# Decay columns by SBUF rows and TensorE, a first block in two groups, and another order of the steps, in a gated linear recurrence with a feed-forward layer

## The chip, the cores and the metric

The kernel runs on one core of a Trainium2 chip. The metric is the device time of one execution in microseconds, the median of several runs; profiles are of one execution each. TensorE (PE) multiplies matrices into PSUM, which has eight banks here. VectorE (DVE), ScalarE (ACT) and GpSimd (POOL) do the elementwise work, SyncE (SP) issues most of the DMAs. Each engine works through its own queue in order.

## The reference

```python
mag = sqrt(a_re*a_re + a_im*a_im)
scale = minimum(mag, 0.999) / (mag + 1e-06)
a_re_n, a_im_n = a_re*scale, a_im*scale
for t in range(S):                       # S = 768
    ar, ai = a_re_n[:, :, t, :, None], a_im_n[:, :, t, :, None]
    new_re = ar*S_re - ai*S_im
    new_im = ar*S_im + ai*S_re
    S_re, S_im = new_re + k[t] (x) v[t], new_im       # outer product, per head
    y[:, :, t] = q[t] @ S_re
x = y, tokens as rows                    # 4 x 768 tokens, 8 heads x 48 = 384 columns
out = (sigmoid(x @ w_gate) * (x @ w_val)) @ w_out     # 384 -> 1536 -> 384
```

There are 4 batches, 8 heads and 48 channels. a is complex, one number for each channel and token.

## The kernel before, in words

The sequence is cut into six blocks of 128 tokens. A slab is one batch in one block, numbered m = 4 x block + batch, so slabs 0 to 3 are the first block, and there are 24. Within a slab the recurrence becomes matrix products: logarithms of the magnitudes and angles are summed along the tokens by a matmul with a triangular matrix; k and q are multiplied by the exponentials and by cosine and sine; q times k gives a masked score matrix, and scores times v give y. A state for each batch carries from block to block, and is multiplied by the decay over a whole block, a number for each channel.

Slabs are prepared in groups, `SIZES` (4, 4, 4, 4, 4, 2, 2). Each piece of work is a step with a name, and `Plan.order` sorts all steps by the due times in the table `TIMES`, then puts them out in that order. So the table is the order of each engine's queue; its numbers do nothing else. `HOME` says by a letter for each step of a kind whether it runs on VectorE (v), GpSimd (g) or ScalarE (a). `SLOTS` gives the buffers, `WARM` puts extra matmuls on zeros ahead of some steps. ScalarE's function tables are loaded where the order needs another one.

The steps, by name:

- per slab: lr, la load a; sq squares it, add adds the two squares; lk, lq, lv load k, q, v; v16 converts v.
- per group: lna (Ln of the real part), inv (Exp of its negative), r (imaginary over real), atan (Arctan); lnm (Ln of the magnitude), lh the cap on it. Groups in `SPLIT` make fp16 pairs (lh, ll; th, tl) in place of fp32 for the two triangular matmuls.
- per slab: cl (triangular matmul of the logarithms), ee (its two exponentials), qke (q and k times ee); ct (triangular matmul of the angles, with the carried angle), r16 and nid (whole turns off), cr (the carry), ab, cs (the two sines); ks, qs (k and q times cosine and sine); tp and qkT (transposes of k and q by TensorE and the copy from PSUM), or xk and xq for slabs in `CROSSED` (the DMA crossbar); sc (scores), mst (mask); kv and P (state update), u (state times decay), x16 (its fp16 copy); y, y16, xp, xt (output, fp16, transposed).
- per pair of slabs: pg and pv (the two feed-forward products, six pieces each, L1058), tanh and p (the gate), po (second product, L1097); then ot and st (evacuation and store).

What the change touches is the way of the block's decay from one row to columns. The last token's row of ee, 384 numbers on one partition, goes to DRAM by scr (L691). When all rows of a group are there, rbe (L698) reads them back by two DMAs with channels on partitions, 48 at partition 0 and 48 at partition 64:

```python
nc.sync.dma_start(
    rbe[p0:p0 + D, c, lo:lo + n],
    scr[c][lo:lo + n].rearrange("b (h d) -> d b h", d=D))
```

Then arr (L707, GpSimd) multiplies a block's columns by those of the block before. u (L955) multiplies the state by arr.

Of the kernel before, what the change touches and what calls it, by code (L numbers as in the profile page):

```python
# [10 lines left out]
ALU = mybir.AluOpType  # L11
# [16 lines left out]
CROSSED = range(9, 24)  # L28
# [3 lines left out]
SPLIT = range(2, 7)  # L32
MSTP = ()
HOME = {
    "sq": "vaaavvvaaaaaaaavaaaaaaaa",
    "add": "vgvvgggggggggggggggggvgg",
    "lh": "gvgggggvvggv",
    "r": "vvgggggggggv",
    "v16": "ggggggvvggggggagvvvavagv",
    "qke": "gggvggggggggggggggggvggg",  # L40
    "th": "aaaavgggvgav",
    "ab": "vaavvaaavaaavvaaaaaaaavv",
    "u": "ggggggggggggggggvvvv",
    "x16": "gggvgaagggvavggg",
    "y16": "vaavavvvaavvavvvaaaaaaaa",
    "xt": "vvavvvvvavvvvvvavavaavav",
    "ot": "avvvaavvavaaavavaavavaaav",
}
SIZES = [4, 4, 4, 4, 4, 2, 2]
TIMES = {  # L50
    "wg": [
        28.88, 44.09, 23.19],
    "wv": [
        31.95, 49.27, 52.96],
    "wo": [
        74.01, 69.87, 76.44],
    "lr": [
        0.75, 10.04, 8.57, 1.12, 10.05, 13.69, 19.93, 24.8, 44.13, 57.38,
        60.18, 62.71, 70.64, 78.81, 78.82, 70.65, 101.57, 120.18, 117.75,
        117.48, 166.56, 168.43, 133.38, 151.46],  # L60
    "la": [
        1.49, 10.03, 8.56, 8.08, 13.7, 10.06, 15.09, 30.65, 47.51, 55.33,
        60.17, 62.72, 70.68, 76.47, 78.45, 78.83, 102.43, 102.49, 117.76,
        107.79, 167.59, 169.97, 134.14, 150.84],
    "sq": [
        7.2, 10.07, 8.67, 8.09, 16.38, 16.39, 19.94, 31.68, 50.55, 58.76,
        60.19, 65.28, 76.49, 78.87, 86.27, 79.55, 103.09, 122.49, 117.77,
        118.73, 171.82, 172.15, 146.69, 151.47],
    "add": [
        8.07, 12.17, 9.54, 8.55, 19.27, 23.18, 31.71, 31.73, 57.18, 63.7,  # L70
        66.74, 66.92, 78.78, 80.37, 92.65, 85.96, 116.2, 126.77, 120.19,
        123.7, 174.48, 175.13, 150.64, 154.3],
    "lna": [
        10.75, 32.78, 65.3, 92.67, 122.97, 176.29, 156.77],
    "lh": [
        12.18, 10.02, 31.66, 31.96, 70.62, 71.44, 98.38, 107.93, 127.81,
        132.62, 179.91, 158.47],
    "lnm": [
        13.71, 32.8, 67.09, 92.7, 127.39, 176.21, 155.21],
    "inv": [  # L80
        12.16, 32.79, 66.3, 92.68, 123.68, 186.68, 160.83],
    "r": [
        14.55, 13.68, 35.36, 35.47, 70.36, 69.88, 102.45, 97.5, 132.59,
        136.16, 188.77, 175.22],
    "cl": [
        17.66, 19.25, 16.37, 15.08, 34.36, 36.17, 41.65, 37.98, 74.07, 75.45,
        78.44, 77.72, 106.6, 105.21, 109.33, 109.12, 135.26, 140.18, 137.85,
        138.18, 181.4, 181.73, 172.62, 160.4],
    "ee": [
        20.75, 21.83, 19.91, 19.26, 41.31, 40.19, 42.81, 41.66, 75.49, 78.85,  # L90
        79.54, 81.56, 108.45, 107.58, 111.51, 109.52, 145.1, 141.4, 140.29,
        141.38, 182.09, 185.02, 176.12, 163.91],
    "scr": [
        32.77, 40.65, 33.65, 41.29, 56.14, 54.7, 49.68, 54.71, 97.53, 88.7,
        86.74, 98.31, 120.16, 123.71, 120.2, 119.68, 150.82, 156.06, 154.25,
        145.08, 191.39, 191.37, 187.65, 179.98],
    "rbe": [
        57.33, 57.39, 98.35, 123.74, 159.31, 200.77, 187.66],
    "lk": [
        19.92, 32.76, 24.68, 21.22, 45.82, 32.81, 49.69, 49.67, 70.66, 86.77,  # L100
        88.69, 98.36, 98.32, 109.16, 125.87, 124.61, 143.56, 98.4, 144.41,
        150.81, 154.27, 187.62, 166.15, 179.69],
    "lq": [
        24.69, 36.86, 30.66, 21.81, 47.5, 42.79, 57.37, 56.15, 76.46, 89.5,
        97.49, 98.41, 98.34, 117.95, 133.31, 124.81, 146.68, 149.99, 166.12,
        152.53, 174.3, 193.31, 179.92, 187.68],
    "lv": [
        23.15, 40.64, 24.67, 33.18, 63.3, 65.89, 76.45, 78.84, 86.76, 97.54,
        100.02, 114.29, 97.52, 133.34, 133.35, 133.82, 157.18, 163.85, 145.05,
        143.75, 196.08, 185.51, 185.52, 201.23],  # L110
    "v16": [
        23.16, 44.12, 31.69, 40.2, 65.29, 65.9, 81.57, 82.21, 102.48, 97.55,
        117.03, 117.49, 117.74, 135.3, 138.51, 140.52, 158.46, 164.82, 174.26,
        166.14, 200.58, 212.8, 200.59, 203.07],
    "qke": [
        24.7, 38.63, 31.7, 21.82, 47.52, 49.28, 58.49, 57.34, 83, 92.66,
        98.39, 99.11, 114.28, 120.21, 133.32, 130.11, 149.81, 154.26, 166.17,
        170.31, 207.38, 195.9, 186.67, 192],
    "atan": [
        17.67, 37.87, 70.84, 102.47, 140.28, 188.79, 179.95],  # L120
    "ct": [
        19.9, 22.34, 18.61, 21.23, 38.62, 42.78, 47.29, 53.38, 79.53, 82.2,
        91.02, 95.63, 110.3, 115.66, 128.44, 122.96, 145.04, 149.23, 162.25,
        163.23, 205.57, 199.59, 185.16, 186.14],
    "r16": [
        20.74, 23.98, 21.21, 22.55, 40.66, 44.71, 49.29, 55.35, 80.39, 82.99,
        93.51, 96.84, 111.3, 117.78, 130.73, 123.75, 145.86, 150.03, 163.24,
        163.84, 205.61, 200.81, 185.68, 186.66],
    "nid": [
        21.8, 28.01, 24.81, 23.14, 41.28, 45.8, 52.13, 55.54, 81.38, 84.69,  # L130
        93.94, 97.48, 111.5, 118.2, 131.37, 127.38, 146.89, 150.63, 163.89,
        166.75, 205.66, 201.64, 186.46, 187.63],
    "cr": [
        23.2, 35.46, 25.06, 24.66, 42.8, 49.24, 57.19, 57.35, 84.66, 91.36,
        97.58, 99.61, 114.27, 120.17, 132.12, 130.09, 149.01, 154.24, 166.76,
        169.5],
    "ab": [
        23.17, 36.83, 31.67, 23.9, 44.08, 46.65, 54.68, 57.2, 82.51, 91.37,
        97.56, 98.51, 112.3, 118.69, 131.73, 130.08, 147.74, 152.52, 166.13,
        170.32, 205.94, 202.02, 187.13, 191.38],  # L140
    "cs": [
        23.89, 36.85, 31.72, 25.46, 45.01, 49.25, 58.48, 57.36, 84.67, 91.38,
        98.37, 99.62, 114.32, 120.96, 132.6, 130.1, 150.83, 154.28, 166.77,
        171.8, 205.95, 203.08, 188.29, 192.65],
    "ks": [
        24.79, 39.92, 31.74, 26.65, 48.59, 49.66, 59.54, 57.59, 84.68, 93.5,
        98.44, 99.97, 116.18, 120.97, 134.13, 132.13, 151.57, 157.16, 167.58,
        174.28, 207.39, 203.34, 191.35, 193.83],
    "qs": [
        25.66, 39.93, 31.75, 28, 49.26, 51.13, 66.73, 61.47, 85.39, 93.95,  # L150
        99.1, 102.21, 116.21, 121.61, 136.15, 132.14, 152.44, 157.17, 169.49,
        174.29, 208.03, 205.62, 191.36, 194.7],
    "tp": [
        26.64, 28.02, 40.18, 40.63, 31.93, 33.19, 30.19, 30.64, 49.88, 50.33,
        61.45, 52.29, 68.26, 70.63, 64.78, 63.69, 88.06, 86.96],
    "qkT": [
        27.39, 28.87, 41.3, 41.67, 32.57, 33.64, 35.35, 31.94, 50.53, 52.97,
        62.09, 54.69, 70.67, 73.22, 66.72, 65.24, 88.85, 88.71],
    "sc": [
        28.89, 31.65, 45.79, 44.72, 35.56, 35, 36.81, 32.58, 53.21, 59.55,  # L160
        62.81, 55.32, 72.09, 80.38, 67.86, 66.91, 96.61, 89.49, 102.2, 103.48,
        117.94, 117.47, 108.78, 111.28, 125.86, 125.64, 134.12, 133.89,
        149.55, 146.67, 149, 141.36, 161.6, 166.11, 163.9, 163.94, 176.11,
        174.25, 179.67, 178.15, 214.75, 214.32, 209.97, 212.79, 197.41,
        196.54, 200.56, 201.24],
    "mst": [
        29.47, 34.24, 46.25, 45.83, 36.82, 36.84, 37.26, 35.45, 55.34, 60.16,
        63.29, 56.11, 78.8, 80.76, 69.85, 69.84, 97.51, 92.69, 104.82, 105.55,
        120.14, 118.22, 111.29, 111.7, 127.15, 130.12, 134.64, 135.25, 151.48,
        147.72, 149.8, 142.24, 162.59, 167.57, 165.19, 164.83, 179.68, 177.51,  # L170
        180.09, 179.97, 215.82, 214.74, 211.5, 213.59, 200.78, 198.31, 202.03,
        201.63],
    "kv": [
        32.75, 45.02, 41.08, 52.74, 74.04, 66.7, 85.43, 95.43, 104.35, 107.57,
        117.73, 118.71, 143.53, 139.97, 149.78, 141.15, 171.76, 168.21,
        180.55, 176.13],
    "P": [
        33.17, 45.81, 44.1, 53.2, 75.48, 67.22, 88.72, 96.62, 107.95, 108.8,
        125.22, 119.67, 145.07, 144.42, 150.86, 144.4, 174.32, 168.61, 181.75,
        179.96],  # L180
    "y": [
        35.34, 52.95, 39.91, 41.45, 65.88, 66.29, 85.49, 85.97, 103.07,
        106.19, 121.6, 118.72, 132.83, 136.14, 152.51, 152.46, 168.42, 166.57,
        182.06, 183.12, 217.78, 216.07, 201.29, 205.6],
    "y16": [
        37.86, 55.55, 41.32, 42.03, 66.71, 69.83, 86.26, 86.73, 104.59,
# [199 lines left out]
def kernel(  # L386
# [184 lines left out]
    for g, n in enumerate(SIZES):  # L571
# [131 lines left out]
        for s in range(n):  # L703
            rbe_key[m0 + s] = key
# [462 lines left out]
```

## Time and profile before

| | before |
|---|---|
| median of 3 runs | 260.3 us (259.03 to 261.05) |
| the profiled execution: own time | 259.69 us |
| its span | 258.0 us |
| mean granted TensorE clock | 0.987 |
| TensorE matmul busy, share | 218.9 us, 85% |
| VectorE, ScalarE, GpSimd busy | 82%, 78%, 51% |
| bytes moved by DMA | 40.26 MB, mean 156 GB/s |
| table loads on ScalarE (in order) | 29, 1.283 us each |

The span is the time from the first to the last instruction of the profile; the execution's own time holds some 1.7 us more. Times in the profile's rows are from the start of the span. In the view by slices each digit is the busy share in tenths of a fortieth of the span. In the view by stage each engine has its busy time and, in brackets, the number of instructions; the last three columns are the granted clock, the DMA share and GB/s. In the view of waits the row is engine, tile and line, then what it waited for, the total, the times and the longest one. Matmuls are pipelined, so their busy times overlap the next one's.

### The profile page before, as it was taken

The numbers are of one execution on the slowest core, as the hardware profiler recorded it, in microseconds if no ns is written. First come the engines' busy times: TensorE is split into PE (matmuls) and PEld (weight loads), VectorE is DVE, ScalarE is ACT, GpSimd is POOL, SyncE is SP. The second block draws the span as 40 slices with busy tenths as digits, with TensorE's granted clock in tenths as the row PEclk, the third lists the DMA queues.
The fourth block names the chain that finished last, engine by engine and source line by source line (L and its number), as shares of the span: only waits on it lengthen the run. The fifth ranks groups of instructions, "written<-read, shape, count | busy, mean of one in ns | idle before, by whom it ended". The sixth has DMA issues, their size and how long they took to land.

```text
span 258.0 us, 5947 instructions
## 1 busy us (share of the span) xinstructions
PE 218.9 (85%) x2249; PEld 168.2 (65%) x2249; DVE 210.4 (82%) x345; ACT 200.8 (78%) x323; POOL 131.0 (51%) x137
## 2 busy tenths in 40 slices
PE   0068278999999869979999899989999999999994
PEld 0034264677888647757767778768667877668882
DVE  3465699899999989997899998988897979868261
ACT  1695999966999669997899997899899894542620
POOL 3229568716996764795979931722924371000000
PEclk9999689999999999999999999999999999999999
DMA  7999994899999968998989799959999659490021
GB/s 147 216 212 197 202 178 76 141 166 117 189 186 188 193 128 147 160 231 191 213 124 218 140 166 207 222 124 110 227 147 227 112 106 163 92 196 31 3 93 61
DMA packets 182988, 40.26 MB, mean 156 GB/s; under 512 B 175880, under 2 KB 182960, under 8 KB 182960
## 3 DMA queue, kind: packets, MB, share of 16 engines
q1 hardware_dynamic: 178816, 36.33, 76.0%
q0 software_dynamic: 4144, 3.56, 9.3%
q8 instruction: 17, 0.28, 0.5%
q14 instruction: 11, 0.09, 0.1%
HBM read 30.77 MB, written 4.78 MB: 138 GB/s over the span
## 4 chain that ended last, share of the span: by engine, by line
PE 29%; DVE 17%; ACT 17%; DMA 16%; issue 8%; SPq 7%; POOL 4%; DVEq 0%; ACTq 0%; POOLq 0%
PE banks L1058 12%; PE banks L1097 8%; ACT L1130 4%; DMA qk<-in_q_dram 4%; DMA a<-in_a_re_dram 3%; DVE p L1076 3%; DMA qkT<-qst 3%; SPq L565 3%; ACT g L1069 3%; DMA v<-in_v_dram 3%; DVE mst L941 2%; SPq L698 2%; DVE kst L864 2%; PE banks L671 2%; DVE qst L864 2%
## 5 line engine op out<-in xcount | busy, mean ns | idle before, releaser
L1058 PE MATMUL banks<-xt,wv 128*128 128x256 f16 x432 | 57.2, 272 | 1.8 <-ACT ot L525 0.9
L1058 PE MATMUL banks<-xt,wg 128*128 128x256 f16 x432 | 55.9, 272 | 1.4 <-DVE p L1076 0.6
L1097 PE MATMUL banks<-wo,p 128*128 128x384 f16 (+1 forms) x300 | 55.6, 319 | 0.5 <-ACT ot L525 0.5
L1069 ACT ACTIVATE g<-banks 128x512 f16<-128x512 f32 x72 | 41.1, 601 | 18.4 <-DVE p L1076 12.5
L1076 DVE SCALAR_TENSOR_TENSOR p<-g,banks 128x512 f16<-128x512 f16 x72 | 48.0, 681 | 8.2 <-ACT g L1069 3.6
L736 POOL TENSOR_TENSOR qk<-qk,ee 128x768 f32<-128x768 f32 x22 | 41.9, 1921 | 13.5 <-DMA qk<-in_q_dram 10.9
L1058 PEld LDWEIGHTS <-wv 128*128 128x128 f16 x432 | 41.0, 98 | 10.0 <-issue 3.6
L1058 PEld LDWEIGHTS <-wg 128*128 128x128 f16 x432 | 41.3, 98 | 9.3 <-issue 2.9
L1097 PEld LDWEIGHTS <-p 128*128 128x128 f16 x300 | 27.9, 97 | 15.3 <-issue 2.1
L1130 ACT ACT_TABLE_LOAD x29 | 37.2, 1283 | 0.5
L604 POOL TENSOR_TENSOR lm<-sq 128x384 f32<-128x384 f32 x20 | 21.5, 1076 | 31.1 <-ACT sq L596 27.0
L941 DVE TENSOR_TENSOR mst<-banks,msk_t 128x512 f16<-128x512 f32 x48 | 32.1, 683 | 4.2 <-PE banks L926 4.1
L864 DVE TENSOR_TENSOR kst<-qk,banks 128x768 f16<-128x768 f32 x24 | 22.7, 947 | 4.1 <-issue 2.0
L671 PE MATMUL banks<-lm,wl_t 128*128 128x384 f32 x16 | 8.6, 653 | 17.3 <-ACT lm L617 15.5
L864 DVE TENSOR_TENSOR qst<-qk,banks 128x768 f16<-128x768 f32 x24 | 22.7, 946 | 0.0
L596 ACT ACTIVATE sq<-a 128x768 f32<-128x768 f32 x19 | 16.0, 847 | 8.0 <-DMA a<-in_a_im_dram 4.4
L660 POOL TENSOR_TENSOR a<-a 128x768 f32<-128x768 f32 x9 | 16.3, 1814 | 6.5 <-PE banks L796 3.3
L926 PEld LDWEIGHTS <-qkT 128*128 128x128 f16 x192 | 13.5, 98 | 7.0 <-issue 3.9
L671 PEld LDWEIGHTS banks<-lm,wl_t 128*128 128x128 f32 x16 | 3.6, 250 | 19.5 <-ACT lm L617 16.5
L811 DVE TENSOR_SCALAR r<-banks 128x384 f16<-128x384 f32 x24 | 13.1, 551 | 3.9 <-PE banks L796 3.3
L828 ACT ACTIVATE cr<-banks 32x384 f32<-32x384 f32 x20 | 9.7, 483 | 8.5 <-DVE banks L843 8.2
L907 PE MATMUL banks<-idn_t,kst 128*128 128x128 f16 x72 | 10.4, 229 | 6.7 <-DVE qst L864 4.6
(90 smaller groups left out, 421.9 us busy)
## 6 DMA issues: line engine op xcount, KB each, us to landing
a<-in_a_re_dram SPq DMA_DIRECT2D x24, 192.0 KB, 4.0
a<-in_a_im_dram SPq DMA_DIRECT2D x24, 192.0 KB, 3.7
qk<-in_k_dram SPq DMA_DIRECT2D x24, 192.0 KB, 3.9
qk<-in_q_dram SPq DMA_DIRECT2D x24, 192.0 KB, 2.8
v<-in_v_dram SPq DMA_DIRECT2D x24, 192.0 KB, 5.2
out_dram<-ot SPq DMA_DIRECT2D x23, 192.0 KB, 2.5
wg<-in_moe_w_gate_dram POOLq DMA_DIRECT2D x3, 384.0 KB, 7.4
wv<-in_moe_w_val_dram POOLq DMA_DIRECT2D x3, 384.0 KB, 5.4
```

What stands on the lines that cost most here:

```text
L596: on.activation(out=T[SQ], in_=T[A][:, :, s], func=FT.Square)
L604: home("add", m).tensor_tensor(out=T[LM][:, s], in0=T[SQ][:, 0], in1=T[SQ][:, 1], op=ALU.add)
L660: home("r", w).tensor_tensor(out=T[A][:, 1, i:j], in0=T[A][:, 1, i:j], in1=T[A][:, 0, i:j], op=ALU.mult)
L671: nc.tensor.matmul(T[CL][:, :HD], wl_t, T[LM][:, s], start=True, stop=True)
L736: home("qke", m).tensor_tensor(out=T[QK], in0=T[QK], in1=T[EE], op=ALU.mult)
L864: nc.vector.tensor_tensor(out=T[SL][i].rearrange("p h (r x) -> p h r x", r=2)[:, :, :, 0:D], in0=heads(T[QK][:, i]).unsqueeze(2) .broadcas ...
L941: nc.vector.tensor_tensor(out=T[MS][:, :n_], in0=T[SC], in1=msk_t.unsqueeze(1).broadcast_to([L, n_, L]), op=ALU.mult)
L1058: nc.tensor.matmul(T[ACC][:, r], wt[:, j, f0:f0 + 128], T[XT][:, :, j], start=(j == 0), stop=(j == 2))
L1069: nc.scalar.activation(out=T[G16], in_=T[PG], func=FT.Tanh, scale=0.5)
L1076: nc.vector.scalar_tensor_tensor(out=T[PT][:, 2 * fp:2 * fp + 2], in0=T[G16], scalar=1.0, op0=ALU.add, in1=T[PV], op1=ALU.mult)
L1097: nc.tensor.matmul(T[PO][:, :wd], T[PT][:, fb, s0:s0 + L], wo16[:, fb, c0:c0 + wd], start=(fb == 0), stop=(fb == NFB - 1))
L1130: nc.scalar.preload_act_table_set(SETS[key[1]])
```

## The change

- The row of ee goes by one DMA from SBUF to SBUF, into eight partitions (one for each head) of `rows_t`. There is no DRAM tile for it.
- A new TensorE step rbt turns a group's rows to columns by two fp32 matmuls with a small identity, into a PSUM bank. The step arr is now on VectorE: it copies the columns to rbe, except in the last block, and multiplies them by those of the block before, except in the first.
- `SIZES` becomes (2, 2, 4, 4, 4, 4, 2, 2): the first block is prepared as two groups of two slabs. `SPLIT` moves by one, so the same slabs have fp16 pairs.
- `CROSSED` starts at slab 12 in place of 9; slabs 9, 10 and 11 are transposed by TensorE.
- The homes of many steps, all due times, buffers and the extra matmuls change. By the letters, squares on GpSimd go from 0 to 11, on ScalarE from 19 to 9.
- Small constants that VectorE makes are put at the head of the ordered part.

In the new order the engines' queues begin like this (number of slab, group or step behind the name):

```
SP    lr0 la0 lr1 la1 lr2 lr3 lk0 la3 la2 lq0 lk1 lq1 lv0 lv2 lr4 lr7 la7 la4 la6 lk2 lq2
      lr6 la5 scr0 lk4 lr5 lv1 lk3 lq4 lq3 scr3 scr2 scr1 lv3
ACT   sq1 lna0 inv0 (table) atan0 (table) lnm0 lna1 inv1 lnm1 ee1 ee0 (table) atan1 cr0 cs0 cr1
      cs1 cr2 ab2 cs2 (table) ee2 sq6 ee3 sq5 lna2 inv2 lnm2 ab3 cr3 (table) cs3
DVE   sq0 r0 lh0 sq3 sq2 add3 r2 r16_1 qke1 r16_0 ab1 ab0 qke0 r16_2 ks0 qs0 ks1 qs1 qkT0 add7
      qke2 ... ks3 qs3 mst2 mst2 r16_4 qkT3 P3 mst3 xt1
PE    ct0 ct1 cl1 cl0 nid1 nid0 cl2 ct2 nid2 cl3 tp0 tp1 tp0 kv0 ct3 tp1 sc1 sc0 tp2 nid3 sc1 cl6
      sc0 tp2 y0 rbt0 kv1 cl5 y1 rbt1 cl4 xp0 ct4 sc2 sc2 cl7 xp1 tp3 kv3 nid4 tp3 kv2 sc3 ct6
      y2 pg(0,0)
```

The core of the diff:

```diff
-CROSSED = range(9, 24)
+CROSSED = range(12, 24)
-SPLIT = range(2, 7)
+SPLIT = range(3, 8)
 HOME = {
-    "sq": "vaaavvvaaaaaaaavaaaaaaaa",
-    "add": "vgvvgggggggggggggggggvgg",
-    "lh": "gvgggggvvggv",
-    "r": "vvgggggggggv",
-    "v16": "ggggggvvggggggagvvvavagv",
-    "qke": "gggvggggggggggggggggvggg",
-    "th": "aaaavgggvgav",
-    "ab": "vaavvaaavaaavvaaaaaaaavv",
-    "u": "ggggggggggggggggvvvv",
-    "x16": "gggvgaagggvavggg",
-    "y16": "vaavavvvaavvavvvaaaaaaaa",
-    "xt": "vvavvvvvavvvvvvavavaavav",
-    "ot": "avvvaavvavaaavavaavavaaav",
+    "sq": "vavvgaagaggagagavaaggggg",
+    "add": "gggvggvvgggggggggggggggg",
+    "lh": "vggggggggggg",
+    "r": "vvggvgggvggg",
+    "v16": "gggaggagggggggaaagggvggv",
+    "qke": "vvvggggggggggggggggggggg",
+    "th": "aaaavvaaggvv",
+    "ab": "vvaaaaaaavaaaavaaaaaavaa",
+    "u": "gggggggggggggggvgggg",
+    "x16": "ggggggggggvgggag",
+    "y16": "vvaaaaaaavavvaaaaavavaaa",
+    "xt": "vvaavvavvvvavvavvvvvaaaa",
+    "ot": "vaaavvavaavavaaaaaavavava",
 }
-SIZES = [4, 4, 4, 4, 4, 2, 2]
+SIZES = [2, 2, 4, 4, 4, 4, 2, 2]
...
 WARM = {
-    ('ct', 3): 8,
-    ('ct', 1): 1,
-    ('sc', 0, 0): 4,
-    ('sc', 0, 1): 10,
-    ('y', 0): 2,
-    ('pv', 1, 0): 4,
-    ('pv', 1, 3): 1,
-    ('cl', 10): 7,
+    ('ct', 2): 6,
+    ('sc', 1, 0): 5,
+    ('cl', 6): 1,
+    ('cl', 5): 2,
+    ('sc', 2, 0): 7,
+    ('cl', 7): 1,
+    ('pg', 1, 0): 1,
+    ('pv', 1, 0): 2,
+    ('pg', 1, 5): 1,
 }
...
+    idf_t = const.tile([32, 32], F32, name="idf_t")
+    rows_t = const.tile([32, len(SIZES), 64], F32, name="rows_t")
+    nc.gpsimd.memset(rows_t, 0.0)
...
-    nc.gpsimd.memset(rbe, 0.0)
...
-            def e(T, EE=EE, b=b, c=c):
-                nc.sync.dma_start(scr[c][b:b + 1], T[EE][L - 1:L, 0])
+            def e(T, EE=EE, s=s, g=g):
+                nc.sync.dma_start(rows_t[H * s:H * s + H, g, :D],
+                                  heads(T[EE][L - 1:L, 0]))

             add(("scr", m), e, after=[("ee", m)], use=[EE])

-        def e(T, c=c, lo=lo, n=n):
-            with nc.allow_non_contiguous_dma(reason="columns of decays"):
-                for p0 in (0, 64):
-                    nc.sync.dma_start(
-                        rbe[p0:p0 + D, c, lo:lo + n],
-                        scr[c][lo:lo + n].rearrange("b (h d) -> d b h", d=D))
-
-        key = add(("rbe", g), e, after=[("scr", m0 + s) for s in range(n)])
+        RB = bank("rb", g)
+
+        def e(T, RB=RB, n=n, g=g):
+            for p0 in (0, 64):
+                nc.tensor.matmul(T[RB][p0:p0 + 64, :H * n], rows_t[:H * n, g],
+                                 idf_t[:H * n, :H * n], start=True, stop=True)
+
+        add(("rbt", g), e, after=[("scr", m0 + s) for s in range(n)], new=[RB])
+
+        def e(T, RB=RB, c=c, lo=lo, n=n):
+            rb = T[RB][:, :H * n].rearrange("p (b h) -> p b h", h=H)
+            if c < NCH - 1:
+                nc.vector.tensor_copy(out=rbe[:, c, lo:lo + n], in_=rb)
+            if c:
+                nc.vector.tensor_tensor(
+                    out=arr[:, c, lo:lo + n], in0=rbe[:, c - 1, lo:lo + n],
+                    in1=rb, op=ALU.mult)
+
+        key = add(("arr", g), e,
+                  after=[("rbt", g)]
+                  + sorted({rbe_key[m0 + s - B] for s in range(n) if c}),
+                  use=[RB])
...
-            def e(T, c=c, lo=lo, n=n):
-                nc.gpsimd.tensor_tensor(
-                    out=arr[:, c, lo:lo + n], in0=rbe[:, c - 1, lo:lo + n],
-                    in1=rbe[:, c, lo:lo + n], op=ALU.mult)
```

## The prediction

> **What bounds it now.** I read the page's busy table and slices first, then busy time by stage, then TensorE's timeline, the chain and the waits.
>
> ```profile
> span 258.0 us, 5947 instructions
> PE 218.9 (85%) x2249; PEld 168.2 (65%) x2249; DVE 210.4 (82%) x345; ACT 200.8 (78%) x323; POOL 131.0 (51%) x137
> PE   0068278999999869979999899989999999999994
> PEclk9999689999999999999999999999999999999999
> ```
> ```profile
> 0.00:49.77 49.77, 25.76 (x211) 16.82 (x212) 34.10 (x65) 38.85 (x53) 28.84 (x38) 0.93 0.93 171
> 49.77:254.20 204.43, 193.10 (x2045) 151.40 (x2040) 176.30 (x281) 161.42 (x270) 102.16 (x100) 1.00 0.85 153
> ```
> ```profile
> 49.77 0.81 PE L1058 MATMUL banks<-xt,wg 128*128 128x256 f16 x6
> ```
> ```profile
> 242.13 3.27 PE banks L1058 x30
> ```
> There are two stages. Up to 49.8 us, where the first feed-forward step (pg) starts, TensorE is half idle and the chain runs through loads, ScalarE and VectorE. From then on TensorE is full. How full must come from its issue spacing, since busy time includes modelled ends: 30 matmuls of 256 columns take 3.27 us, so a pg or pv step of six takes 0.653. A po step takes the same; tp takes 0.45, sc 0.22, kv 0.20, y 0.41 (0.22 in the first block), xp 0.165, nid 0.16, cl 0.32 (fp32 0.645), ct likewise plus 0.7 where the carry is added. 144 pg and pv make 94.0, po 48.0, ct 13.1, sc 10.6, cl 10.3, y 9.1, tp 8.1, kv 4.0, xp 4.0, nid 3.8: 204.9 us. In the written order 18.1 lie before the first pg, 186.8 behind it. From 49.8 to TensorE's end at 254.2 are 204.4 us, so 17.6 of stalls are spread over the second stage, none over 2 us. A tail of 3.8 (last evacuation and store) ends the span. The sum is **49.8 + 186.8 + 17.6 + 3.8 = 258.0**; 1.69 around it makes that execution's 259.69, a little below the median of 260.3.
>
> **The decays' path.** What goes:
>
> ```profile
> PE banks L671 <- ACT lm L617: 15.5, 1, 15.5
> POOL arr L707 <- DMA rbe<-scr: 20.9, 4, 8.3
> ```
> ```profile
> rbe<-scr SPq DMA_DIRECT2D x10, 6.0 KB, 4.2
> ```
> ```profile
> q1 hardware_dynamic: 178816, 36.33, 76.0%
> ```
> Fourteen column DMAs vanish (24 KB x 10 read as 4-byte pieces: 18,432 packets, 10% of q1's), with 0.3 to 3.1 us of SP's time each. GpSimd's 20.9 us of waits for them end. But GpSimd is 51% busy, and of TensorE's waits only one (1.7 us, y for x16) hangs on it; the earned time is 0 to 2, I take 1. DMA also loses six of 30 crossbar transposes. By the packets' times (8.9 ns a piece of 4 bytes; 1,024 pieces of 25.7 ns a transpose; 16 engines) each of the two is 10 us of DMA time. DMA share in the second stage is 0.85, so landings shorten; I count that only in the stall range below.
>
> What comes: per group one rbt step of two tiny fp32 matmuls. The nearest row is the carry's fp32 matmul with 32 stationary rows (L801): 182 ns per weight load, two passes each. Four loads bound it at 0.73, full overlap at 0.1; I take 0.3, 2.4 us for eight. VectorE gets 12 copies and products of up to 32 columns, 0.24 each by GpSimd's row (arr, 241 ns): 2.9 us, off the path.
>
> **The wait it adds.** rbt now stands in TensorE's queue, where nothing overtakes it, and waits for a row DMA in SP's queue. Behind it stand, group by group in the new order: kv 1; cl 4; pv (1,0); ct 9; po 4; pg (7,3); pg (9,1); po 16, and on VectorE behind arr y16, p, r16, ks. A row DMA has no landing row; the column DMAs' 2.6 to 5.8 (median 4.2) are nearest, and the carry's small ones land in 2.7 to 3.1: I take 3. TensorE work between the last row's issue and rbt, in the order: 0, 2.3, 1.3, 0.6, 4.0, 0, 2.0, 11.7 us. That alone would leave up to 13 us of waits. What covers it is that SP runs ahead of its place in the order: scr of slab 8 is issued at 95.4 while TensorE's steps of that place run near 108; scr of slab 16 at 161.3 against 166; of slab 17 at 170.1 against 172. A lead of 2 to 12 leaves a wait at group 5 (0 to 2) and at group 0; I take 1 for the former. If stores waiting for ot hold SP back (22.5 us of its waits are that), the cover is gone and the full price falls due.
>
> **Crossbar from slab 12.** Slabs 9 to 11 return to TensorE: 6 tp of 0.45 = **+2.7 us**, all in the full stage, and 6 qkT copies of 0.685 = 4.1 on VectorE. SP loses six issues and their 3.5 us landings.
>
> **The new homes** (counts times row means): VectorE −6.5 us net with the 4.1 and 2.9 included (u −2.1, v16 −2.6, ab −1.7, lh −2.2, y16 −1.6, x16 −1.5, others); ScalarE about even (10 squares less, −8.5; more ab, th, y16, xt, v16; one table load more, 1.28); GpSimd +25 (11 squares of 1.8), to some 156. None becomes the bound: they stay under 85% of the span, TensorE's needed work is above 80% and gains 5.
>
> Here a rule speaks against the change. The Trainium skill, SBUF — State Buffer, "SBUF: two separate sides", says that GpSimd and a VectorE operation with two SBUF inputs share a port pair as an exclusive lock, the loser blocked for the whole instruction. The trace has it:
>
> ```profile
> L736 DVE TENSOR_TENSOR qk<-qk,ee x2: 949/1391/1833, 23.1 to 226.2; 128x768 f32<-128x768 f32 x2
> ```
> 0.949 late, when GpSimd is idle, 1.833 at 23.1 beside GpSimd's own multiply. By the rule 20 us more on GpSimd block more. But exposed VectorE operations (two SBUF inputs, or copies within SBUF) fall from 49 to 37; at GpSimd's 51 and 60% that is 25 against 22 meetings: by count no loss, by the rule alone up to 11 x 0.9 = 10 us of VectorE time, which its 6.5 less and its idle share hide mostly. In the sum 0; in the head each VectorE qke is taken at 1.83.
>
> **The first block in two groups** is the gain. Walk of the new order with the rows' durations: the first four loads land by 6.5 (as now); square on ScalarE to 7.3; Ln and Exp of 768 columns (0.84 each; now 1.48) to 9.05; table 1.28, Arctan to 11.15; table, Ln, then group 1's Ln, Exp, Ln to 15.8; two ee pairs to 17.4; table, Arctan to 19.5; cr and cs of slabs 0 and 1 to 22.2. VectorE in between: r16, qke, r16, ab, ab, qke to 21.7, so ks 0 at 21.7, where now it is 28.65, and the first transposes at 23.5 for 30.5. Slabs 2 and 3 follow: cs 2 to 24.1, table, ee, squares, group 2's Ln, Exp, Ln to 33.2, table, cs 3 to 36.4; ks 3, qs 3 to 39.3, then mst, mst, r16, qkT, P, mst, xt on VectorE: pg at **43.1**. Against it stands rbt 0: its row (slab 1) is behind scr 3 in SP's queue, which waits for ee 3 at 27.9 and two q loads; issued about 32.5, landed about 36, that delays y 1 and y16 1 some 1.4 us: **44.5**, ends 43 and 47 (loads saturate the DMA there: share 0.93).
>
> The clock: between 27.4 and 34.2 the granted clock was 0.50, around TensorE's gap of 4.6. The Trainium skill, TensorE: Matmul & The Clock Gate, "What's actually happening", says cold is half speed and it takes some 3.4 us of sustained work to lift. The new order has 26 warming matmuls for 37. By the trace the phase falls before pg and costs nothing; by the rule, if it meets pg, 3.4 us of work at half speed cost 3.4. I take 0 and keep 3.4 for the range.
>
> **Sum.** Start −5.3; TensorE's work behind it 191.3 for 186.8 (2.7 + 2.4, less what moved ahead of pg): +4.5; y wait −1; group 5's wait +1; the remaining stalls: of some 16, four (0.5 to 1.4 us, nid and tp behind VectorE) go by VectorE's 6.5 less, I take −3. Together −3.8, and 259.7 − 3.8 = 255.9: **256.0 us**, own range 252 to 259.5 (start −1.5/+2.5, stalls ±3).
>
> **Rivals.** (1) *Shorter landings free the second stage.* With 20 of some 220 us of DMA time gone, stalls fall from 17.6 to about 10: 44.5 + 191.3 + 10 + 3.8 + 1.7 = 251. For: share 0.85. Against: direct TensorE waits for DMA total 1.6 us. Chance 0.15. (2) *Cancelled.* The 4.5 added and the start's gain cancel, stalls stay at 17.6, start 45: 259.4, within 1% (about what a measurement of this kernel can tell from no change). For: TensorE is the bound of the second stage, and no part shortens its work. 0.22. (3) *TensorE waits at rbt.* SP has no lead, the row lands 4.2 behind its issue: groups 2 to 6 pay 2.9, 3.6, 0.2, 4.2, 2.2 = 13 at most, 8 with three of them: 264 (up to 269). Slower once they pay over 7. For: SP's waits for ot, and rows due right before rbt. Against: the leads above. 0.18. That it doesn't do what it says is excluded by the diff. Forecast 0.45.
>
> The forecast's own range lies nine tenths below −1%; so faster 0.55, same 0.25, slower 0.20. Range 249 to 264: rival 1's centre is in, the dear half of rival 3 out.
>
> **To be seen after.** First L1058 near 44.5; ks 0 near 22; no rbe DMA, DMA share of the second stage below 0.8; rbt waits of TensorE under 3 us in total; GpSimd near 156, VectorE near 204. Wrong if pg starts after 47, or rbt leads TensorE's waits.

## The result, and the profile after

The changed kernel takes **251.4 us** (median of 4 runs, 249.74 to 253.07) against 260.1 (259.03 to 261.05) in the same comparison: ratio **0.967 [0.958, 0.975]**, 8.6 us less. Where an experiment's profile fell on one of its longer runs, its time below comes from the ratio, and the profile shows only what waited for what.

The page of the kernel after, its head, two of its rows by slices and one DMA queue (q1: packets, MB, share of 16 engines):

```profile
span 251.4 us, 6100 instructions
PE 224.3 (89%) x2318; PEld 173.2 (69%) x2318; DVE 206.3 (82%) x341; ACT 201.6 (80%) x330; POOL 150.6 (60%) x152
...
PE   0167789999989799999999999999999979999994
...
PEclk9997799999999889999999999999999999999999
...
q1 hardware_dynamic: 154160, 34.68, 66.8%
```

TensorE has 69 instructions more (48 for six tp, 32 for eight rbt, 11 extra matmuls fewer), and still the span is 6.6 us shorter. GpSimd has 19.6 us more work, VectorE 4.1 less, and q1 24,656 packets less. The nines of TensorE begin earlier, and there is a new weak clock around slices 14 and 15.

The same by stage, cut where the first pg starts:

```profile
0.00:45.88 45.88, 28.08 (x221) 17.54 (x222) 35.03 (x71) 39.20 (x57) 26.83 (x36) 0.93 1.01 189
45.88:248.20 202.32, 196.24 (x2104) 155.68 (x2099) 171.27 (x271) 162.03 (x274) 123.81 (x117) 0.99 0.72 146
```

The first stage is 3.9 us shorter, and its DMA is now full all through (1.01 for 0.93). In the second stage the share fell from 0.85 to 0.72.

TensorE's end is at 248.2, and 3.2 us of tail follow. With the prediction's own count of work (191.3 behind the first pg) the profiled sum reads 45.9 + 191.3 + **11.0** + 3.2 = 251.4 (rounded), where before it was 49.8 + 186.8 + **17.6** + 3.8. So the start gave 3.9, the tail 0.6, the added work by that count took 4.5, and the stalls, which are what is left of the sum, gave 6.6. This profiled execution (253.07 with what lies around it) is the longest of the four. The four fall in two pairs, 253.1 and 252.5 at a mean clock of 0.978, 249.7 and 250.3 at 0.993. By these means TensorE ran some 11 us at half clock in the first pair and some 3.5 in the second (an estimate), so the 2.8 us between the pairs go with the clock.

All that TensorE waited for in the second stage:

```profile
PE banks L794 <- DVE a L779: 2.4, 2, 1.8
PE banks L794 <- DVE a L520: 1.2, 1, 1.2
PE banks L905 <- DVE state L981: 1.1, 1, 1.1
PE banks L971 <- DVE p L1074: 0.4, 1, 0.4
PE banks L924 <- DVE qst L862: 0.3, 1, 0.3
PE banks L971 <- ACT g L1067: 0.2, 1, 0.2
PE banks L905 <- ACT g L1067: 0.2, 1, 0.2
```

Seven rows with 5.8 us, for 14 rows with 10.7 before. Gone are the wait for x16 on GpSimd (1.7), for y (1.3), for r16 (1.5), for ot (1.4) and for the transposing DMAs (1.6). New on top is ct (L794), which waits for the fp16 pair of the angles. **L693, the new rbt, is not in the list**, so by this view TensorE never waited for a row DMA. The listed waits fell by 4.9 us; the rest of the 6.6 is in gaps that the view gives to no releaser, or in the count of work.

### The profile page after: what moved, and what is told of

Its sections match the earlier page's. It is cut to its first block, busy times and chain, and to the rows that moved or that the text cites. A ratio compares the mean times of both kernels' runs of the same rounds, so it can differ in the third digit from the quotient of the medians.

```text
span 251.4 us, 6100 instructions
## 1 busy us (share of the span) xinstructions
PE 224.3 (89%) x2318; PEld 173.2 (69%) x2318; DVE 206.3 (82%) x341; ACT 201.6 (80%) x330; POOL 150.6 (60%) x152
## 4 chain that ended last, share of the span: by engine, by line
PE 45%; ACT 6%; POOL 3%; DVE 3%; issue 1%; DMA 1%; SPq 0%; DVEq 0%; POOLq 0%
PE banks L1056 22%; PE banks L1095 14%; PE banks L924 2%; DVE a L779 2%; POOL a L653 1%; PE banks L794 1%; DMA a<-in_a_re_dram 1%; ACT L1138 1%; PE banks L1031 1%; PE banks L668 1%; PE banks L999 1%; PE banks L997 1%; PE banks L971 1%; POOL qk L734 1%; ACT g L1067 1%
## 5 line engine op out<-in xcount | busy, mean ns | idle before, releaser
L1074 DVE SCALAR_TENSOR_TENSOR p<-g,banks 128x512 f16<-128x512 f16 x72 | 48.1, 680 | 13.3 <-ACT g L1067 6.8
L1056 PE MATMUL banks<-xt,wg 128*128 128x256 f16 x432 | 56.6, 273 | 0.1
L1056 PEld LDWEIGHTS <-wv 128*128 128x128 f16 x432 | 40.6, 98 | 6.5 <-issue 0.2
L734 POOL TENSOR_TENSOR qk<-qk,ee 128x768 f32<-128x768 f32 x21 | 39.5, 1884 | 8.8 <-DMA qk<-in_q_dram 5.4
L1095 PEld LDWEIGHTS <-p 128*128 128x128 f16 x300 | 27.8, 98 | 13.3 <-issue 0.6
L597 POOL TENSOR_TENSOR lm<-sq 128x384 f32<-128x384 f32 x21 | 21.8, 1046 | 12.9 <-DVE sq L591 8.2
L591 POOL TENSOR_TENSOR sq<-a 128x768 f32<-128x768 f32 x11 | 17.1, 1558 | 14.2 <-DMA a<-in_a_im_dram 11.2
L794 PE MATMUL banks<-a,wt_t 128*128 128x384 f32 x16 | 9.4, 693 | 12.7 <-ACT a L741 11.6
L653 POOL TENSOR_TENSOR a<-a 128x768 f32<-128x768 f32 x8 | 14.5, 1816 | 4.4 <-ACT a L647 4.4
L912 DVE COPY qkT<-banks 128x1024 f16<-128x1024 f16 x24 | 16.1, 681 | 0.8 <-PE banks L906 0.8
L905 PE MATMUL banks<-idn_t,kst 128*128 128x128 f16 x96 | 13.6, 224 | 2.3 <-DVE state L981 1.1
L906 PE MATMUL banks<-idn_t,qst 128*128 128x128 f16 x96 | 13.5, 224 | 0.6 <-DVE qst L862 0.6
```

The lines of the kernel that those rows point to most:

```text
L591: on.tensor_tensor(out=T[SQ], in0=T[A][:, :, s], in1=T[A][:, :, s], op=ALU.mult)
L597: home("add", m).tensor_tensor(out=T[LM][:, s], in0=T[SQ][:, 0], in1=T[SQ][:, 1], op=ALU.add)
L653: home("r", w).tensor_tensor(out=T[A][:, 1, i:j], in0=T[A][:, 1, i:j], in1=T[A][:, 0, i:j], op=ALU.mult)
L734: home("qke", m).tensor_tensor(out=T[QK], in0=T[QK], in1=T[EE], op=ALU.mult)
L1056: nc.tensor.matmul(T[ACC][:, r], wt[:, j, f0:f0 + 128], T[XT][:, :, j], start=(j == 0), stop=(j == 2))
L1074: nc.vector.scalar_tensor_tensor(out=T[PT][:, 2 * fp:2 * fp + 2], in0=T[G16], scalar=1.0, op0=ALU.add, in1=T[PV], op1=ALU.mult)
```

## The experiments

All are the changed kernel with one thing altered, except e8, which is the kernel before. Where an alteration needs it, the buffers' table and the due times of the altered steps were fitted; the other due times are those of the change. Ratios are to the kernel before on the same chip.

**Four slabs in the first group again (e1).**

```diff
-SIZES = [2, 2, 4, 4, 4, 4, 2, 2]
+SIZES = [4, 4, 4, 4, 4, 2, 2]
-SPLIT = range(3, 8)
+SPLIT = range(2, 7)
```

The first Arctan is now the group's, due at 19.31, and ct, r16, nid of slabs 0 and 1 stand behind it.

> The kernel after, with the first block again as one group of four slabs (the steps of slabs 0 and 1 that need the Arctan of the first group wait for that of the whole group); all else, order and homes too, as in the kernel after. Theory A (the start earns its part): ks 0 comes 3 to 6 us later, the first feed-forward step moves from 45.9 to 49 or 50, and the time is 254 to 257 us. Rival (the start is covered by later work, the gain is in the second stage): 251 to 252.5 us.

Ratio 1.000 [0.994, 1.006]: the whole gain gone, more than either side had forecast. ks 0 starts at 32.0 and pg at 55.5, which is later than in the kernel before; behind it stand 203.9 us to TensorE's end, 1.6 more than in the change. But the start holds a loss that four slabs need not have. SP's waits from 20 to 50 us:

```profile
SPq L581 <- ACT ee L575: 10.3, 1, 10.3
```

The row DMA of slab 0 keeps its early place in SP's queue, its exponential now comes late, and the loads behind it stand for 10.3 us. So e1 overstates the part.

**The same with an order nearer to it (e5):** Arctan ahead of the exponentials (15.453), the square of slab 3 on ScalarE, slab 0's row DMA due at 33.28 for 25.85.

> The first block as one group of four slabs, as in the first experiment, with an order of its own at the start: Arctan before the exponentials, the square of slab 3 on ScalarE, and the row of slab 0 later in SP's queue so that loads do not wait behind it. Theory A (the two groups earn about 4 us at the start; of the 9.6 us by which the first feed-forward step moved before, the rest came from an order not made for it): first feed-forward step at 48.5 to 51, time 255 to 258 us. Rival (four slabs in one group cost the whole 9 us wherever the steps stand): step at 54 or later, 261 to 264 us.

0.996 [0.991, 1.002], 7.4 us over the change and somewhat past what theory A allowed. ks 0 comes at 27.4, pg at 51.6. From there to TensorE's end it is 203.6 us, against 202.3 in the change. TensorE's first pg in e5, its timeline:

```profile
51.63 1.47 PE L954 MATMUL banks<-xt,wg 128*128 128x256 f16 x12
```

So against this kernel the two groups bring pg 5.7 us ahead, and nothing of that is given back behind it. That this order is as good as four slabs could have is not shown: the kernel before, with four slabs and its own order, has pg at 49.8, only 3.9 behind the change.

**Decays by DRAM again, in the new order (e2).** The diff's row and rbt parts are undone; the rbe DMAs take the place of rbt.

> The kernel after, with the decays again through DRAM: row DMA to DRAM, two column DMAs by group right behind the last row in SP's queue, the product on GpSimd at the same place of the order; no rbt on TensorE. Theory A: TensorE loses 2 us of work, GpSimd gains waits, and one or two TensorE stalls of 2 us come back: 250.5 to 253.5 us. Rival B (the column DMAs, by load and SP's time, made most of the 6.6 us of stalls that went): 255 to 258 us, stalls of the second stage back at 15 or more.

1.000 [0.995, 1.005], 8.4 us over the change (0.032 of 262), more than both forecasts. pg is at 46.8, so nearly all of the loss is in the second stage. All waits from 45 us on, two of the rows:

```profile
POOL arr L599 <- DMA rbe<-scr: 12.4, 2, 6.6
DVE kst L756 <- POOL qk L628: 9.4, 3, 5.2
```

GpSimd stands for the columns, but first ahead of arr at 66.1, and TensorE's longest stall ended at 57.7. That stall in TensorE's timeline, GpSimd's timeline ahead of it, and SP's waits from 20 to 60 us:

```profile
57.73 1.79 PE L950 MATMUL banks<-xt,wv 128*128 128x256 f16 x12 [4.27 <-DVE qst L756]
```
```profile
50.99 1.47 POOL L490 TENSOR_TENSOR sq<-a 128x768 f32<-128x768 f32 x1 [5.51 <-DMA a<-in_a_im_dram]
```
```profile
SPq L590 <- DMA scr<-ee: 6.0, 3, 2.4
```

SP waits for the rows to land in DRAM before it reads them back, twice before 35 us, and the loads behind come late: it issues three imaginary parts of a from 45.0, in the change from 37.9. GpSimd's square waits 5.5 us for one of them, its qke come late, ks on VectorE waits 5.2 for those, and TensorE 4.3. So this stall came by SP's wait for the row and the loads behind it, not by the columns. Whether the columns cost TensorE anything later is not shown.

**Crossbar from slab 9 in the new order (e3)**, the transposes right behind ks and qs.

> The kernel after, with slabs 9 to 11 again transposed by the DMA crossbar. Theory A (TensorE's work is the bound of the second stage): 2.7 us less work on it, 4.1 less on VectorE: 248.5 to 250.5 us. Rival B (crossbar load on the DMA engines and late landings cost more than the work): 252.5 to 255 us, with waits of sc for qkT.

1.019 [1.010, 1.027]: slower than the kernel before and than both forecasts, though TensorE has 2.7 us less to do. Its waits from 45 us on sum to 18.5 us (5.8 in the change's second stage), and only 0.6 of that is for a transposed tile, which was rival B's sign. SP's waits from 80 to 130 us, then SP's own timeline:

```profile
SPq L779 <- DVE kst L758: 16.7, 2, 12.0
```
```profile
84.62 0.87 SPq L454 DMA_DIRECT2D qk<-in_q_dram  x1
97.52 1.35 SPq L779 DMA_TRANSPOSE qkT<-kst  x1
98.92 0.57 SPq L454 DMA_DIRECT2D a<-in_a_re_dram  x1
```

Between two loads SP does nothing for 12 us but wait for ks. So I set these six transposes some 6 us later in the order **(e6)**.

> Crossbar from slab 9, as in the third experiment, but with the six transposes 6 us later in SP's queue. Theory L (that kernel lost its time because SP, which runs ahead of its order, stood 12 us at a transpose whose k was not ready, and every load behind it came late): 249 to 254 us, SP's wait at the transposes under 6 us. Rival B (the crossbar's load on the DMA engines costs it): 261 us or more again.

0.999 [0.994, 1.005]. That is 5 us better than e3 but short of what I expected. From 80 to 130 us SP's wait for ks fell from 16.7 to 5.1, and that for qs is 0.7, as theory L had it, but most of the loss stayed; GpSimd waits 7.8 us for one load of q, up to 127.1. So taking most of the standing still away gave back some 5 of the 13 us. Whether these transposes cost by their DMA time or by any place that I gave them stays open.

**All three undone (e4)**, homes and due times kept.

> The kernel after with all three of its parts undone (one group of four slabs, decays through DRAM, crossbar from slab 9): what stays of the change is the order of the steps and their homes. Theory A (start and order both earn): 253 to 257 us. Rival C (the three parts earn all of it and the order nothing): 259 to 261 us. Rival D (order and homes earn all of it): 250 to 252 us.

1.069 [1.059, 1.079]: 27 us over the change, with pg at 55.1, far from all three forecasts. The losses of e1, e2 and e3 (8.4, 8.4 and 13.3) are each as large as the whole gain. Such numbers are not what the parts are worth; the runs below say what they hold.

**The rows alone in the kernel before (e8)**: rows by SBUF, rbt just ahead of arr, arr on VectorE at its old place.

> The kernel before with the new path of the decays alone (row DMA from SBUF to SBUF, rbt on TensorE, copy and product on VectorE at the place of the old product); groups, crossbar, homes and order as before. Theory A (the path relieves SP and GpSimd, TensorE gains 2 us): 258 to 261 us. Theory W (relief of SP's queue counts in any order): 253 to 257 us. Rival 3 of the prediction (TensorE waits at rbt): 263 us or more, with waits of TensorE for the row DMAs.

1.044 [1.036, 1.051], 11 us slower than before. That is rival 3's time without its mechanism: TensorE waits 0.6 us at rbt, and none of it for a row DMA. All waits of e8, the leading row:

```profile
POOL state L859 <- DVE arr L609: 26.8, 4, 10.8
```

The work is the same as in the change. But arr now stands in VectorE's queue behind rbt in TensorE's, and at the old places both come late for GpSimd: its arr had waited 20.9 us for the columns, and now its state step waits 26.8 for arr. Not all of the 11 us need lie there: pg is at 52.8, 3.1 later than before, and TensorE is at half clock from 27.0 to 40.6 (before: 27.4 to 34.2).

**The DMA load without the data path (e7).** The change plus two column DMAs a group, of 4-byte pieces, into a tile that nobody reads, placed behind the group's row DMAs.

```diff
+        def e(T, lo=lo, n=n, g=g, c=c):
+            with nc.allow_non_contiguous_dma(reason="load alone"):
+                for p0 in (0, 64):
+                    nc.sync.dma_start(
+                        junk[p0:p0 + D, g, :n],
+                        q[lo:lo + n, :, c * L].rearrange("b h d -> d b h"))
+
+        add(("ld", g), e)
```

> The kernel after with two column DMAs by group added, in 4-byte pieces as the kernel before had them, from q into a tile that nothing reads; nothing waits for them except their turn in SP's queue. Theory Q (the DRAM path cost by SP's waits for the row in DRAM and what was queued behind, not by its load): 251 to 254 us. Rival (10 us of DMA time by the small pieces, and SP's issue time, is what costs): 257 us or more, near the second experiment.

0.994 [0.990, 0.998]: 6.8 us over the change by the ratios, 6.4 by the profiled spans of e7 and f1_after_again (258.5 and 252.1). That is the rival's time. pg still starts at 45.5. How sixteen DMAs that nobody waits for reach TensorE can be read down three engines. GpSimd in the change, at its sq and the next weight load:

```profile
44.41 1.46 POOL L591 TENSOR_TENSOR sq<-a 128x768 f32<-128x768 f32 x1
45.82 0.82 POOL L543 DMA_DIRECT2D wv<-in_moe_w_val_dram  x1
```

GpSimd in e7, the same two:

```profile
48.67 1.47 POOL L489 TENSOR_TENSOR sq<-a 128x768 f32<-128x768 f32 x1 [4.56 <-DMA a<-in_a_im_dram]
50.08 0.82 POOL L441 DMA_DIRECT2D wv<-in_moe_w_val_dram  x1
```

TensorE in e7, and the window behind that stall (the clock is third from the end):

```profile
55.63 2.74 PE L962 MATMUL banks<-xt,wv 128*128 128x256 f16 x12 [3.42 <-DMA wv<-in_moe_w_val_dram]
```
```profile
55.60:59.00 3.40, 3.37 (x18) 2.47 (x19) 1.95 (x4) 0.27 (x1) 2.38 (x3) 0.50 1.42 170
```

SP issues the four added DMAs of the first two groups from 29.4 to 32.1, some of the loads behind them take it longer too (one of v 2.4 us, for 0.4), and the three imaginary parts of a go out from 42.2, in f1_after_again from 37.7. So a load of a lands late, GpSimd's square waits 4.6 us for it, the weight load queued behind that square goes out 4.3 us later, TensorE waits 3.4 us for the weights and then runs 3.4 us at half clock, which costs 1.7 more. That is 5.1 us. It is not an exact account of the 6.4, since f1_after_again has one such window behind pg (at 85.6) and e7 a second (at 209.2).

**The change itself (f1_after_again)** was run once more beside the three kernels that follow, so that they can be compared with it: 0.968 [0.963, 0.973].

> The kernel after, unchanged, on the same chip as the experiments that are compared with it: every theory expects its ratio to the kernel before at 0.96 to 0.975.

**The same load from the fourth group on (f3).**

```diff
+        if g > 2:
+            add(("ld", g), e)
```

> The kernel after with the added column DMAs of the load experiment, but for groups 3 to 7 alone (block 2 on), where the DMA share is 0.72; none in the first 78 us, where it is near 1. Theory G (the small pieces cost where the DMA engines are full, by the loads behind them in SP's queue): within 1.5 us of the kernel after. Rival (they cost everywhere alike): 3 to 5 us slower than it, five eighths of that experiment's loss.

0.970 [0.963, 0.976], beside 0.968 for the change in the same comparison. Ten of the sixteen DMAs, with two thirds of the pieces, cost nothing that can be measured; the DMA share where they fall is 0.7 to 0.9. By difference the six of the first three groups, where the share is 1, cost all of it. Whether that is because of the share, or of what waits behind them on SP in that stretch, is not separated.

**Later places for the ct that wait longest (f2):** ct of slabs 8, 9, 22 and 23, with r16 and nid, 1 to 3 us later in the order.

> The kernel after, with the four angle sums ct of slabs 8, 9, 22 and 23 two or three us later in the order (and their r16 and first nid): TensorE stood 2.5 us at the first two, 1.9 at the last two, with other work queued behind. Theory S (a step put in TensorE's queue ahead of its operand's landing stops the engine, and the same step later costs nothing; the half-clock window that follows the first gap goes too): 2 to 5 us faster than the kernel after. Rival (what hangs on ct comes later by as much): within 1 us of the kernel after.

0.980 [0.973, 0.987], some 3 us slower than the change. TensorE's timeline in f2, a stall that now stands at nid:

```profile
91.37 0.48 PE L712 MATMUL banks<-r,nid_t 128*128 128x384 f16 x1 [1.70 <-DVE r L705]
```

The stall moved to a step that needs ct, and the list of f2's second stage has other waits too (1.8 us for weights, 1.6 for p). My reading that ct merely stood too early in TensorE's queue fell.

**SP's order alone (f4).** Due times of SP's steps shifted at random by up to 1.5 us: 103 of 197 DMAs change their place, by six places at most; every other queue keeps its order, and the buffers' table is fitted. It is one draw.

> The kernel after with SP's order alone disturbed: each due time of SP's DMAs moved by up to 1.5 us at random between its operands and its users, 103 of 197 DMAs at another place, at most six places away; nothing else changes. Theory P (a place in SP's queue matters where something waits behind it, and undoing one part in a finished order costs several us by places alone): 3 us or more slower than the kernel after. Rival (the order is tolerant, and what the undone parts cost is their own): within 1.5 us of it.

1.002 [0.997, 1.007], 9 us over the change, with pg at 46.7. The whole gain is gone, with all three parts in. TensorE's waits behind pg sum to 13.6 us, for 6.4 in f1_after_again, and it has one more window at half clock. The two leading ones:

```profile
PE banks L696 <- DVE a L422: 4.3, 1, 4.3
PE banks L826 <- DMA qkT<-kst: 3.3, 2, 2.9
```

And VectorE's row before the first of them:

```profile
86.95 2.39 DVE L422 TENSOR_SCALAR a<-a 128x768 f16<-128x768 f32 x1 [3.55 <-DMA a<-car]
```

GpSimd waits 4.7 us for a load of v (0.75 in f1_after_again), so its DMA of the carry, queued behind, goes out at 83.6 (there at 78.3), the carry lands late, and ct waits for its fp16 form. In e1 to e4 many steps stand where they were put for other neighbours; f4 shows that this alone can cost as much as those undone parts seemed worth.

## Why the prediction was right, and where it was not

The direction and the range (249 to 264) held, and so did what was to be seen of pg, ks 0, the DMA share and rbt. The size did not: a fall of 3.8 us was forecast and 8.6 was measured, and 251 was rival 1's figure.

**The start: −3.9 for −5.3.** The mechanism holds: with two groups ks 0 starts at 22.5 (walked: 21.7) and the first transposes at 24.3 (23.5). pg came at 45.9, 1.4 later than 44.5. That distance flatters the walk: 44.5 held 1.4 for rbt 0, where TensorE did not wait, so by luck two errors met, and the walked path of 43.1 was 2.8 too short. 0.8 were lost by ks 0, the rest behind it: the sines of slab 3 ended at 36.9 (walked: 36.4), but VectorE had copies and state steps of slabs 0 to 2 in its queue ahead of ks 3 and began it here, where the walk had ks 3 and qs 3 done:

```profile
39.28 0.95 DVE L862 TENSOR_TENSOR kst<-qk,banks 128x768 f16<-128x768 f32 x1
```

The part is worth 3.9 us of pg against the kernel before and 5.7 against e5 (nearly the same homes), and e5 shows that it passes to the end. This is the step that the runs show best.

**The added work: +4.5 as taken.** One rbt, the change's TensorE timeline, beside SP's issue of group 0's last rows:

```profile
36.06 0.29 PE L693 MATMUL banks<-idf_t,rows_t 16*64 16x16 f32 x4
```
```profile
28.03 2.06 SPq L684 DMA_DIRECT2D rows_t<-ee  x3
```

Four matmuls in 0.29 us, as the 0.3 had it. The instruction count agrees with six tp more. The 4.5 is worked out from such rows; no run measures it by itself.

**The wait at rbt: 0 for +1.** Rival 3 did not happen. SP's lead is in the timeline: the last rows of the groups behind the first block went out by 48.1, 83.0, 127.4 and 162.4, and their rbt ran at 58.3, 89.4, 137.1 and 166.7; the end of the last two groups' issues, 202.7, stands before 209.6. No margin is under 4 us. The walk had slab 1's row issued at 32.5, and it went at 28.0 to 30.1. e8 shows the other side of this step: at places where rbt and arr come late, it is GpSimd that waits for the path, not TensorE at rbt. The prediction asked only whether TensorE would wait.

**The stalls: the term that was mis-sized.** The sum had −1 for y, +1 for group 5 and −3 for the rest, and it was −6.6. I had derived the 3 from VectorE's lighter load, 6.5 us less; VectorE's busy time fell by 4.1. What fell were waits of every kind, those for GpSimd, ScalarE and DMA among them. Rival 1 had set the stalls at about 10 and the time at 251, and its numbers were the better ones. Its mechanism is half shown. DMA load did matter, but not where the prediction had looked for it: f3 puts the load back into the later blocks without loss. What e7 lost goes back to DMAs issued before 55 us, through the queues of SP and GpSimd to a weight load, and e2's longest stall came the same way, by SP's wait for a row in DRAM. f4 shows that the stalls depend on SP's order as much as on any part. How much of the 6.6 the removed DMAs gave, and how much the new order or the new homes, can't be told from these runs: each part was undone in an order made for all three, no run changes the homes alone, and f4 is a single draw.

**Two costs taken as nothing were not.** The port lock is one. The change's timeline at 200 us, GpSimd's multiply, VectorE's step for the fp16 pair (tl) beside it, and TensorE's ct behind it:

```profile
200.19 1.80 POOL L734 TENSOR_TENSOR qk<-qk,ee 128x768 f32<-128x768 f32 x1 [0.40 <-ACT ee L678]
200.24 2.57 DVE L779 SCALAR_TENSOR_TENSOR a<-a 128x768 f16<-128x768 f32 x1
...
202.86 0.32 PE L794 MATMUL banks<-a,wt 128*128 128x384 f16 x1 [1.77 <-DVE a L779]
```

GpSimd ran from 200.19 to 201.99, VectorE's step ended 0.82 later, at 202.81. The same step at 84.98, with no such neighbour, took 0.96. This is the longest stall of the second stage. The form's mean, by the groups of lines of the change:

```profile
L779 DVE SCALAR_TENSOR_TENSOR a<-a 128x768 f16<-128x768 f32 x8 | 11.2, 1394 | 0.3 <-POOL a L520 0.2
```

It was 1.027 us before. So the rule that the prediction weighed (Trainium skill, SBUF — State Buffer, "SBUF: two separate sides") bears on this change: 2.9 us of VectorE's time in this form, and by the 1.6 that the step took longer nearly all of TensorE's 1.8. The count of meetings could say how often they happen, but not that one would stand just before a step that TensorE awaits. The head's qke, taken at 1.83, ran at 0.952.

The other is the clock. It was 0.5 from 18.3 to 21.8 and from 28.6 to 32.0, ahead of pg, as the prediction had it; and again from 86.6 to 90.0, in the full stage, behind two stalls of ct for the carried angle. The change's TensorE timeline there:

```profile
85.99 0.32 PE L794 MATMUL banks<-a,wt 128*128 128x384 f16 x1 [0.67 <-DVE a L779]
86.16 1.04 PE L1056 MATMUL banks<-xt,wg 128*128 128x256 f16 x6
86.99 1.49 PE L1095 MATMUL banks<-wo,p 128*128 128x384 f16 x4
```

Four po matmuls took 1.3 us from one start to the next step's, twice the usual 0.65. Together that window cost some 1.7 us, which is in the 11.0 of stalls. The forecast had kept 3.4 for one, twice too much: 3.4 us at half clock lose half of that. It lies behind waits of 1.2 and 0.7 us between 83.8 and 86.0. It need not come in every execution: the mean of 0.993 in two of the runs leaves room for one such window in all, where this execution had two ahead of pg alone, and f3, with nearly the same two waits (1.1 and 0.7), has none behind pg.

**Where the two errors met.** The start was 1.4 too good in the forecast, the stalls 3.6 too dear, the tail 0.6 too long, which makes the 2.8 between 255.9 and the profiled 253.07. The median, 251.4, lies another 1.7 lower, which goes with the clock. The count of work was taken as it stood, so an error in it would be in the stalls. One size was misread without effect on the sum: the column DMAs' row has 6.0 KB, not 24. What was off was how much of TensorE's idle time would go.

No version here beats the change.

## What to carry to other kernels

Where one in-order queue issues nearly every DMA, ask what stands behind a DMA while it waits, on that queue and on those that its late data hold up: here other places alone cost 9 us (f4). Small-piece DMAs cost 6.4 us when they also stood in the full stretch at the start (e7), and nothing in the later blocks (f3), so take them out of the full stretch first. Preparing less at first so that the bound engine starts earlier is a gain that passed to the end here. A part undone in an order made with it shows the part and the misfit of the order together, so measure the misfit by itself, with several jitters of the order, before giving each part a price.

## What the runs showed of the hardware that was not expected

- After a stall of TensorE in the full stage, a window of 3.4 us at half clock (0.50) often followed: after 3.4 us in e7 (55.6 to 59.0), after 4.3 in e2 (58.7 to 62.2), after 4.3 and 2.9 in f4 (90.4 to 93.9, 182.6 to 186.0), and after 1.2 and 0.7 in the change (86.6 to 90.0). Each costs 1.7 us on top of the stall. In f3 waits of 1.1 and 0.7 us at the same place were followed by none, so the length of a wait does not settle it alone.
- In the change the row DMAs of 1.5 KB took SP mostly 0.65 us to issue, but once 3.3; a load of 192 KB took 3.7 at 50.4, where the DMA share was about 1, and others 0.4. Issue time on SP is not a constant of the DMA's size.
- In f4 the fp16 form of the carried angle took 2.39 us, for 0.56 in the change, beside two GpSimd multiplies from 85.06 on. It reads one tile of SBUF and writes another. A short step can lose three times its length in such a meeting.
